# A fused sparse-attention and mixing kernel: the first batch's token sum in another order of terms, and the later weights' high parts rounded on ScalarE

## The chip, the cores and the metric

The kernel runs on one NeuronCore of a Trainium2 chip. The metric is the device time of one execution in microseconds (us). Before the change three executions took 988.09, 993.77 and 994.96 us (median 993.77). Engines are named as the profile names them: PE is TensorE, DVE is VectorE, ACT is ScalarE, POOL is GpSimd, SP is the engine that issues the DMAs.

## The reference, cut to what matters

```
# attention: 4 batches x 8 heads, 576 tokens, head dim 64
scores = q @ k.T / 8
kth = the 32nd largest score of each row
attn = softmax(scores where scores >= kth, else -1e9)
x = concat over heads (attn @ v)                  # 4 x 576 x 512

# first mixing block
theta = x @ w_theta
yr = einsum('ts,bsd->btd', w_tok_r, x * cos(theta))
yi = einsum('ts,bsd->btd', w_tok_i, x * sin(theta))
u = x + yr + yi                                   # "the token sum"
x = u + relu(u @ w_ch)

# second block
u, v = halves of relu(x @ w_in)
v = w_spatial @ layernorm(v) + b_spatial
out = (u * v) @ w_out
```

The weights of the first block and `w_in`, `w_out` arrive as 64-bit floats; q, k, v, `w_spatial` and `b_spatial` as 32-bit.

## The kernel before, in words

**Attention.** There are 16 visits (4 batches times 4 pairs of heads) of 9 tiles each, 144 tiles of 128 query rows by 576 keys. A tile goes through PE (`ps_s`, L429, two-part products), ACT (copy `x` out of PSUM, L433), DVE (the 32nd largest of each row, two tiles at a time: maximum and minimum of halves, L448 and L449, each with two inputs in SBUF, then MAX8 and MATCH_REPLACE8, L452 to L461, with one input), ACT (`sg` = Sign and `x` = Exp, L480 and L481), POOL (`sg` = their product, L482), PE (transpose `ps_t`, L491), ACT (`ptb`, L492) and PE (product with the values, `ps_v`, L513). Two tiles make a group; DVE is through a group in some 8.6 us while the weights are being split.

**The blocks behind it.** Each matrix product is made of three (`mm3`, L552 to L554): high part times high part, high times low, low times high, where the high part is the operand rounded to the matmul's type and the low part what is left. For the token sum, the sum over the 576 tokens is nine terms k of 128 rows: k = 0 to 3 are token tiles 0 to 3 of x·cos (tiles `zah`, `zal`; weights `tr`), k = 4 to 7 the same tiles of x·sin (`zbh`, `zbl`; weights `ti`), k = 8 the last 64 tokens of both (`zb`; weights `t9`). In the first batch, tiles 0, 1 and 2 go through `Front.rotate` first, and tiles 3 and 4 (the terms 3, 7 and 8) in a second call just before `middle`. The token sum has eight PSUM results (four channel chunks, two halves of the tokens), with three PSUM buffers `ps_m`.

**The weights.** `split_weights` loads each weight in parts, turns 64-bit words into 32-bit floats on DVE (L147, L148, L149; ACT's Abs at L150 and Sign at L154 test the range), rounds the high part (L193), subtracts it (L194) and writes both to DRAM (L204, L205). Seven larger parts of `th`, `tr`, `ti`, `t9` come first (`split_first`), then 21 parts of `ch`, `iv`, `iu`, `sp`, `s5`, `ou` with 512 or 576 columns (`split_rest`), of which 16 are 64-bit. They are recorded one to a group of attention tiles, and what is left after group 21 there. The blocks load each weight back into four large buffers `w` (L264); a load waits until the weight that held its buffer has been used for the last time in that batch.

**The order.** Work is recorded with priorities; a scheduler at build time then fixes one order of instructions for each engine. At run time each engine, and SP's queue of DMAs, goes through its list in that order.

Of the kernel before, what the change touches and what calls it, by code (L numbers as in the profile page):

```python
# [13 lines left out]
AF = mybir.ActivationFunctionType  # L14
OP = mybir.AluOpType
# [9 lines left out]
def sparse_attention_then_moe_kernel(  # L25
# [37 lines left out]
    NFIRST = 4  # L63
# [11 lines left out]
    act, dve, pool, pe = nc.scalar, nc.vector, nc.gpsimd, nc.tensor  # L75

    def f32(ap):
        return ap.bitcast(F32)
# [44 lines left out]
    def is_double(w):  # L123
        return w.dtype == mybir.dt.int64

    def words(w):

        return w.bitcast(I32).rearrange("k (n t) -> k n t", t=2)
# [11 lines left out]
    def double_to_f32(raw, f, exact, i):  # L140


        u = f.bitcast(I32)
        p, n = f.shape
        low, high = raw[:, :, 0], raw[:, :, 1]
        hf = high.bitcast(F32)
        dve.tensor_scalar(u, high, 3, 0x3FFFFFFF, op0=OP.logical_shift_left, op1=OP.bitwise_and)  # L147
        dve.scalar_tensor_tensor(u, low, 29, u, op0=OP.logical_shift_right, op1=OP.bitwise_or)  # L148
        dve.scalar_tensor_tensor(u, high, -(1 << 30), u, op0=OP.bitwise_and, op1=OP.bitwise_or)  # L149
        act.activation(hf, hf, AF.Abs)  # L150
        if exact:
            dve.scalar_tensor_tensor(f, hf, 2.0 ** -15, f, op0=OP.is_ge, op1=OP.mult)
        else:
            act.activation(hf, hf, AF.Sign, bias=smallest[0:p], accum_out=inside[0:p, 0, i:i + 1])  # L154
            pool.memset(inside[0:p, 1, i:i + 1], float(n))

    def split_weights(names, slots, step, exact, first):


        parts = []  # L160
        for n in names:
            parts += [(n, 0, 1)] if SIZE[n] == WID[n] else [(n, c, step) for c in range(0, 4, step)]

        def load(i):
            if i >= len(parts):
                return
            name, c, k = parts[i]
            raw, f, _ = slots[i % len(slots)]
            n = WID[name]
            if name == "t9":  # L170
                where = [(slice(0, 64), 0, w_rT[512:S]), (slice(64, 128), 0, w_iT[512:S])]
            elif name == "s5":
                where = [(slice(0, 64), 0, w_spT[512:S]), (slice(64, 65), 0, b_sp)]
            else:
                where = [(slice(0, 128), j, SRC[name][(c + j) * 128:(c + j + 1) * 128]) for j in range(k)]
            cols = slice(512, 1024) if name == "iv" else slice(0, n)
            for p, j, src in where:
                if is_double(src):
                    nc.sync.dma_start(raw[p, 2 * j * n:2 * (j + 1) * n].rearrange("p (n t) -> p n t", t=2),
                                      words(src)[:, cols])  # L180
                else:
                    nc.sync.dma_start(f[p, j * n:(j + 1) * n], src[:, cols])

        def finish(i):
            name, c, k = parts[i]
            n = k * WID[name]
            _, f, hi = slots[i % len(slots)]
            p = 65 if name == "s5" else 128
            f, hi = f[0:p, 0:n], hi[0:p, 0:n]
            if name == "th":  # L190

                pool.tensor_scalar(f, f, 1.0 / (2.0 * math.pi), 0.0, op0=OP.mult, op1=OP.add)
            pool.tensor_scalar(hi, f, 1.0, 0.0, op0=OP.mult, op1=OP.add)  # L193
            pool.tensor_tensor(f.bitcast(F32R), f, f32(hi), op=OP.subtract)  # L194
            hi = f32(hi)
            c = slice(c * WID[name], c * WID[name] + n)
            if name == "s5":
                for h in (slice(0, 64), slice(64, 128)):
                    nc.sync.dma_start(scratch[name, "h"][h], hi[0:64])
                nc.sync.dma_start(scratch[name, "l"][0:64], f[0:64])  # L200
                nc.sync.dma_start(scratch[name, "l"][64:65], hi[64:65])
                nc.sync.dma_start(scratch[name, "l"][65:66], f[64:65])
            else:
                nc.sync.dma_start(scratch[name, "h"][:, c], hi)  # L204
                nc.sync.dma_start(scratch[name, "l"][:, c], f)  # L205

        load(0)
        load(1)
        for i, (name, c, k) in enumerate(parts):
            yield  # L210
            raw, f, _ = slots[i % len(slots)]
            n = k * WID[name]
            src = {"t9": w_rT, "s5": w_spT}.get(name, SRC.get(name))
            if is_double(src):
                p = 65 if name == "s5" else 128
                double_to_f32(raw[0:p, 0:2 * n].rearrange("p (n t) -> p n t", t=2), f[0:p, 0:n],
                              exact, first + i)
            finish(i)
            load(i + 2)

    def split_first(exact):
        slots = []
        for raw, f in (("zah", "F"), ("zal", "zbh")):
            hi = wts.tile([128, 4 * S], F32R, name="w_hi", tag="w", bufs=WBUF)
            slots.append((big.tile([128, 4 * S], I32, name="w_raw", tag=raw),
                          big.tile([128, 4 * S], F32, name="w_f", tag=f), hi))
        return split_weights(ORDER[:NFIRST], slots, 2, exact, 0)

    def split_rest(exact):
        raw = big.tile([128, 2, 2 * S], I32, name="w_raw", tag="ph")  # L230
        f = big.tile([128, 4, S], F32, name="w_f", tag="pl")
        slots = [(raw[:, i], f[:, 2 * i], f[:, 2 * i + 1].bitcast(F32R)) for i in range(2)]
        return split_weights(ORDER[NFIRST:], slots, 1, exact, 10)

    ORDER = ["th", "tr", "ti", "t9", "ch", "iv", "iu", "sp", "s5", "ou"]

# [79 lines left out]
    def run(exact):  # L316
# [234 lines left out]
        def mm3(out, ah, al, bh, bl, first, last):  # L551
            pe.matmul(out, ah, bh, start=first, stop=False)  # L552
            pe.matmul(out, ah, bl, start=False, stop=False)  # L553
            pe.matmul(out, al, bh, start=False, stop=last)  # L554

        def mps(shape):
            return psum.tile(shape, F32, name="ps_m", bufs=3)
# [190 lines left out]
        FR = {}  # L748
# [28 lines left out]
        def middle(b):  # L777
# [7 lines left out]
            th, tl = (r + i + n for r, i, n in zip(*(W.get(b, n) for n in ("tr", "ti", "t9"))))  # L785
            for c in range(4):
                d = slice(c * 128, (c + 1) * 128)
                for m in halves:
                    p = mps([128, HALF])
                    for k in range(9):  # L790
                        mm3(p, *FR[b].z(k, d), th[k][:, m], tl[k][:, m], k == 0, k == 8)
                        if k == 4:
                            yield 1850
                    udve.tensor_tensor(F[:, c, m], p, F[:, c, m], op=OP.add)
                    lag.step(lambda c=c, m=m: ew.split(F[:, c, m], uh[:, c, m], ul[:, c, m]))
                    yield 1500
# [11 lines left out]
            first = True  # L808
            for m in halves:
                for e in range(4):  # L810
                    p = mps([128, HALF])
                    es = slice(e * 128, (e + 1) * 128)
                    if m is halves[1] and e == 0 or first:
                        lag.flush()
                        first = False
# [72 lines left out]
            for m in halves:  # L888
                for f in range(4):
                    fs = slice(f * 128, (f + 1) * 128)  # L890
                    p = mps([128, HALF])
# [34 lines left out]
        N = len(tiles)  # L926
        work = None
        conv = chain([split_first(exact), split_rest(exact)])
        preps = [iter(())]
        prep_first()  # L930
# [51 lines left out]
        def block(b):  # L982

            if b:
                gap = last(b - 1)
                yield from islice(gap, 4 if b == 1 else 0)
                yield from front(b)
                yield from gap
            else:
                yield from front(b)  # L990
            yield from middle(b)
# [79 lines left out]
```

## Time and profile before

| | |
|---|---|
| three runs | 988.09, 993.77, 994.96 us |
| profiled execution | 986.55 us, span 984.8 us |
| busy over the span | PE 87%, DVE 85%, ACT 64%, POOL 55% |
| DVE busy, 100 to 300 us (of 200) | 195.6 us |
| DVE idle before 800 us, after the start-up | some 26 us |
| DVE busy, 800 to 850 us (of 50) | 9.3 us |
| PE busy, 800 to 985 us (of 185) | 175.0 us |
| the 21 late parts are split | from 118 to 313 us |
| first batch's token sum | from 252 to 310 us |

An engine's busy time counts its instructions from start to end; where an instruction waits for something that no semaphore shows, the wait is inside its duration. The granted clock (PEclk) is a share of TensorE's full speed.

### The profile page before, as it was taken

What the parts mean: (1) busy time and instruction counts of PE and PEld (TensorE: products, weight loads), DVE (VectorE), ACT (ScalarE), POOL (GpSimd) and SP (SyncE); (2) the same over time, 40 slices, a digit from 0 to 9 for tenths busy, and PEclk for the clock granted to TensorE, in tenths of its full rate; (3) what the DMA queues carried; (4) which work ended last, traced back from release to release, by engine and by line L of the source; (5) the groups of instructions that cost most, each with busy time, mean ns of one, the idle gap of its engine ahead of it and who ended that gap; (6) DMA issues with size and microseconds to landing.
All of it is one profiled execution on the core that took longest, in us unless ns stands there. A gap on an engine that the chain in (4) does not pass through costs nothing.

```text
span 984.8 us, 17792 instructions
## 1 busy us (share of the span) xinstructions
PE 854.1 (87%) x5802; PEld 785.8 (80%) x5802; DVE 837.5 (85%) x2710; ACT 626.2 (64%) x1298; POOL 546.2 (55%) x476
## 2 busy tenths in 40 slices
PE   3656677785898999898998999799899999999997
PEld 2555666664797988897898998698889998889987
DVE  6999999899999998899999998999999951463552
ACT  5666767678767567777867777577957764350121
POOL 1686776658685854758385656375655553420030
PEclk9865676687899999999999999899999999999999
DMA  7797774647638463544461844352742645341221
GB/s 218 222 333 224 238 220 150 171 139 203 219 105 241 164 167 140 157 150 100 147 162 32 276 152 144 126 161 71 229 138 68 258 155 181 156 181 52 103 86 53
DMA packets 79393, 159.76 MB, mean 162 GB/s; under 512 B 36143, under 2 KB 40239, under 8 KB 71866
## 3 DMA queue, kind: packets, MB, share of 16 engines
q1 hardware_dynamic: 79290, 158.53, 51.0%
q8 instruction: 48, 0.79, 0.3%
q14 instruction: 55, 0.45, 0.1%
HBM read 108.63 MB, written 23.32 MB: 134 GB/s over the span
## 4 chain that ended last, share of the span: by engine, by line
DVE 46%; PE 32%; ACT 7%; DMA 7%; issue 4%; POOL 3%; SPq 1%; DVEq 0%; ACTq 0%; POOLq 0%
DVE mm L449 8%; PE ps_m L552 7%; DVE mx L458 7%; PE ps_m L553 7%; PE ps_m L554 7%; DVE mm L461 7%; DVE z L452 5%; DVE mm L448 4%; PE ps_v L513 4%; PE ps_s L429 2%; PE ps_t L491 2%; DVE F L568 2%; DMA q<-hi 2%; DVE z L448 2%; DVE cf L471 2%
## 5 line engine op out<-in xcount | busy, mean ns | idle before, releaser
L482 POOL TENSOR_TENSOR sg<-x,sg 128x576 f32<-128x576 f32 x144 | 213.0, 1495 | 150.9 <-ACT x L481 90.9
L513 PE MATMUL ps_v<-vc,ptb 128*128 128x65 f32 (+1 forms) x1280 | 176.6, 277 | 15.1 <-ACT ptb L492 15.1
L513 PEld LDWEIGHTS ps_v<-vc,ptb 128*128 128x128 f32 (+1 forms) x1280 | 167.4, 201 | 24.4 <-ACT ptb L492 18.5
L491 PE MATMUL ps_t<-ident,sg 128*128 128x128 f32 x648 | 132.0, 305 | 42.2 <-POOL sg L482 33.5
L480 ACT ACTIVATE sg<-x,cf 128x576 f32<-128x576 f32 x144 | 103.8, 769 | 56.0 <-DVE cf L471 53.2
L491 PEld LDWEIGHTS ps_t<-ident,sg 128*128 128x128 f32 x648 | 93.7, 166 | 53.9 <-POOL sg L482 39.0
L458 DVE MAX8 mx<-mm 128x8 f32<-128x160 f32 x432 | 118.9, 313 | 0.0
L433 ACT ACTIVATE x<-ps_s 128x576 f32<-128x576 f32 x144 | 92.4, 642 | 32.0 <-POOL sg L482 16.8
L429 PE MATMUL ps_s<-k,q 128*128 128x288 f32 x256 | 91.2, 367 | 24.1 <-ACT x L433 15.0
L552 PE MATMUL ps_m<-w_t,zah 128*128 128x288 f32 (+2 forms) x272 | 98.7, 363 | 11.3 <-DVE F L568 6.7
L481 ACT ACTIVATE x<-x,cf 128x576 f32<-128x576 f32 x144 | 108.0, 767 | 0.1
L492 ACT ACTIVATE ptb<-ps_t 128x640 f32<-128x640 f32 (+1 forms) x144 | 92.4, 642 | 13.2 <-PE ps_t L491 12.3
L554 PE MATMUL ps_m<-w_t,zal 128*128 128x288 f32 (+2 forms) x272 | 96.6, 355 | 0.6 <-DVE zal L568 0.4
L553 PE MATMUL ps_m<-w_t,zah 128*128 128x288 f32 (+2 forms) x272 | 96.5, 355 | 0.0
L452 DVE MAX8 z<-mm 128x8 f32<-128x312 f32 (+1 forms) x288 | 89.5, 372 | 1.9
L552 PE MATMUL ps_m<-w_t,zbh 128*128 128x288 f32 x288 | 85.9, 301 | 3.2 <-DVE F L568 1.9
L461 DVE MATCH_REPLACE8 mm<-mx,mm 128x160 f32<-128x160 f32 x288 | 87.0, 309 | 0.0
L553 PE MATMUL ps_m<-w_t,zbh 128*128 128x288 f32 x288 | 85.4, 300 | 0.6 <-DMA w_t<-d_spl 0.6
L554 PE MATMUL ps_m<-w_t,zbl 128*128 128x288 f32 x288 | 84.3, 299 | 1.0 <-POOL zbl L568 1.0
L552 PE MATMUL ps_m<-ph,w_t 128*128 128x288 f32 x256 | 76.8, 301 | 8.1 <-DMA w_t<-d_chh 4.3
L429 PEld LDWEIGHTS ps_s<-k,q 128*128 128x128 f32 x256 | 55.8, 218 | 33.1 <-ACT x L433 24.6
L449 DVE TENSOR_TENSOR mm<-x 128x576 f32<-128x576 f32 x72 | 82.2, 1141 | 0.0
(175 smaller groups left out, 2391.4 us busy)
## 6 DMA issues: line engine op xcount, KB each, us to landing
k<-hi SPq DMA_DIRECT2D x60, 144.0 KB, 2.6
kl<-raw SPq DMA_DIRECT2D x60, 144.0 KB, 3.1
vc<-in_v_dram SPq DMA_DIRECT2D x48, 128.0 KB, 2.8
w_t<-d_trh SPq DMA_DIRECT2D x4, 1152.0 KB, 5.2
w_t<-d_trl SPq DMA_DIRECT2D x4, 1152.0 KB
out_dram<-t SPq DMA_DIRECT2D x32, 144.0 KB, 2.2
raw<-in_q_dram SPq DMA_DIRECT2D x15, 288.0 KB, 3.0
q<-hi SPq DMA_DIRECT2D x30, 144.0 KB, 2.8
```

The costliest lines, as they stand in the source:

```text
L429: pe.matmul(o, q, k[:, m], start=a == 0, stop=a == len(terms) - 1)
L449: dve.tensor_tensor(mm[:, :, mid:hi], a, b, op=OP.min)
L452: dve.max(out=z[:, i, QUARTER + 8 * k:QUARTER + 8 * k + 8], in_=mm[:, i, losers])
L458: last = dve.max(out=top[i], in_=src[i])
L461: dve.match_replace(out=mr[i], in_to_replace=top[i], in_values=src[i], imm_value=NEG)
L481: act.activation(x, x, AF.Exp, bias=cf[:, 0:1], scale=0.125)
L482: pool.tensor_tensor(sg, x, sg, op=OP.mult)
L491: pe.transpose(pt[:, c, :], x[:, lo:lo + 128], ident)
L513: pe.matmul(o, pt[:, c, q], chunks[:, c, slot], start=alone and c == 0, stop=not alone and i == 1 and c == 3)
L552: pe.matmul(out, ah, bh, start=first, stop=False)
L553: pe.matmul(out, ah, bl, start=False, stop=False)
L554: pe.matmul(out, al, bh, start=False, stop=last)
```

## The change

In the first batch (`b == 0`) the nine terms of each PSUM result of the token sum are taken as 0, 1, 2, 4, 5, 6, 3, 7, 8; in the other batches as before. The generator hands back control after the sixth term instead of the fifth. For the 21 parts of `split_rest`, the rounding of the high part is an ACT activation (Copy) instead of a POOL tensor_scalar; the seven first parts stay on POOL.

```diff
-    def split_weights(names, slots, step, exact, first):
+    def split_weights(names, slots, step, exact, first, late):
...
-            pool.tensor_scalar(hi, f, 1.0, 0.0, op0=OP.mult, op1=OP.add)
+            if late:
+                act.activation(hi, f, AF.Copy)
+            else:
+                pool.tensor_scalar(hi, f, 1.0, 0.0, op0=OP.mult, op1=OP.add)
             pool.tensor_tensor(f.bitcast(F32R), f, f32(hi), op=OP.subtract)
...
-        return split_weights(ORDER[:NFIRST], slots, 2, exact, 0)
+        return split_weights(ORDER[:NFIRST], slots, 2, exact, 0, False)
...
-        return split_weights(ORDER[NFIRST:], slots, 1, exact, 10)
+        return split_weights(ORDER[NFIRST:], slots, 1, exact, 10, True)
...
-                    for k in range(9):
-                        mm3(p, *FR[b].z(k, d), th[k][:, m], tl[k][:, m], k == 0, k == 8)
-                        if k == 4:
+                    terms = range(9) if b else (0, 1, 2, 4, 5, 6, 3, 7, 8)
+                    for i, k in enumerate(terms):
+                        mm3(p, *FR[b].z(k, d), th[k][:, m], tl[k][:, m], i == 0, i == 8)
+                        if i == 5:
                             yield 1850
```

The scheduler makes another order of it on every engine. Line numbers of the changed kernel are higher by 4 to 6 from here on.

On POOL, around the fifth and sixth late part, the order before was this (`w_f` is the part, `sg` the attention's product):

```order
L193 TENSOR_SCALAR w_f<-w_f 128x512
L194 TENSOR_TENSOR w_f<-w_f 128x512
L482 TENSOR_TENSOR sg<-x,sg 128x576 x2
L193 TENSOR_SCALAR w_f<-w_f 128x512
L194 TENSOR_TENSOR w_f<-w_f 128x512
L482 TENSOR_TENSOR sg<-x,sg 128x576 x2
```

and now is:

```order
L486 TENSOR_TENSOR sg<-x,sg 128x576 x2
L198 TENSOR_TENSOR w_f<-w_f 128x512
L486 TENSOR_TENSOR sg<-x,sg 128x576
L198 TENSOR_TENSOR w_f<-w_f 128x512
L486 TENSOR_TENSOR sg<-x,sg 128x576 x3
```

The rounding is gone, and the subtraction, which stood ahead of its group's two products, now stands behind one or both of them.

On ACT, around the fifth late part, before:

```order
L480 ACTIVATE sg<-x,cf 128x576 x2
L481 ACTIVATE x<-x,cf 128x576
L492 ACTIVATE ptb<-ps_t 128x512
L150 ACTIVATE w_raw<-w_raw 128x512
L481 ACTIVATE x<-x,cf 128x576
```

and now:

```order
L484 ACTIVATE sg<-x,cf 128x576 x2
L437 ACTIVATE x<-ps_s 128x576
L485 ACTIVATE x<-x,cf 128x576 x2
L150 ACTIVATE w_raw<-w_raw 128x512
L195 ACTIVATE w_f<-w_f 128x512
L496 ACTIVATE ptb<-ps_t 128x512
```

The new copy (L195) stands behind the part's Abs (L150), here behind both Exp of the group; at the sixth part one Exp stands behind it.

On PE, at the first three results of the token sum, before (`w_t_1121` and `w_t_1123` are `tr`, `w_t_2418` and `w_t_2420` are `ti`), after the terms 0, 1, 2 of all three:

```order
L552 MATMUL ps_m_2764<-w_t_1121,zah_905 128x288
L553 MATMUL ps_m_2764<-w_t_1123,zah_905 128x288
L552 MATMUL ps_m_2616<-w_t_1121,zah_905 128x288
L553 MATMUL ps_m_2616<-w_t_1123,zah_905 128x288
L552 MATMUL ps_m_2725<-w_t_1121,zah_905 128x288
L553 MATMUL ps_m_2725<-w_t_1123,zah_905 128x288
```

and now, after the terms 0, 1, 2 of the first two:

```order
L556 MATMUL ps_m_2616<-w_t_2418,zbh_2263 128x288
L556 MATMUL ps_m_2725<-w_t_2418,zbh_2263 128x288
L495 MATMUL ps_t_2593<-ident_75,sg_2564 128x128
L557 MATMUL ps_m_2616<-w_t_2420,zbh_2263 128x288
L557 MATMUL ps_m_2725<-w_t_2420,zbh_2263 128x288
```

PE goes on with term 4, which needs the weights `ti`, where it took term 3, which needs token tile 3. The fourth result's first matmul stands at place 789 of PE's instructions before and 806 now; the first matmul with `ch` stands at place 1012 in both. Of the 5,059 instructions of PE in this pass 1,040 stand behind the last one of the attention, in both.

## Rows read from the trace of the kernel before

**Rows 1.** The page, part 1: busy us (share of the span) xinstructions.

```profile
PE 854.1 (87%) x5802; PEld 785.8 (80%) x5802; DVE 837.5 (85%) x2710; ACT 626.2 (64%) x1298; POOL 546.2 (55%) x476
```

**Rows 2.** Busy time by stretches; each number is busy us (xinstructions).

```profile
core 0: us, PE busy (x) PEld busy (x) DVE busy (x) ACT busy (x) POOL busy (x), PEclk, DMA share, GB/s
...
150.00:200.00 50.00, 38.23 (x182) 32.77 (x183) 46.96 (x169) 35.39 (x75) 30.80 (x26) 0.64 0.55 161
250.00:300.00 50.00, 45.83 (x333) 42.97 (x332) 49.27 (x153) 34.58 (x68) 37.23 (x35) 0.96 0.50 160
...
800.00:850.00 50.00, 49.18 (x340) 44.66 (x339) 9.27 (x45) 21.44 (x52) 21.44 (x23) 1.00 0.43 163
```

**Rows 3.** POOL's late parts: line 193 (ns min/median/max, first and last start us).

```profile
L193 POOL TENSOR_SCALAR w_f<-w_f x21: 608/758/1177, 120.5 to 307.4; 128x512 fp32r<-128x512 f32 x16, 128x576 fp32r<-128x576 f32 x4, 65x576 fp32r<-65x576 f32 x1
```

**Rows 4.** Groups of ACT, shapes apart: xcount | busy us, mean ns | idle before.

```profile
L568 ACT ACTIVATE zbh<-vt 128x512 fp32r<-128x512 f32 x12 | 7.3, 626 | 9.0 <-POOL vt L568 9.0
```

**Rows 5.** Timeline at the fifth late part: start us, us, engine, line; [idle before].

```profile
159.16 1.44 ACT L480 ACTIVATE sg<-x,cf 128x576 f32<-128x576 f32 x2 [1.01 <-DVE cf L471]
...
159.42 0.68 DVE L149 SCALAR_TENSOR_TENSOR w_f<-w_raw,w_f 128x512 int32<-128x512 int32 x1
...
160.19 0.76 POOL L193 TENSOR_SCALAR w_f<-w_f 128x512 fp32r<-128x512 f32 x1 [3.43 <-DVE w_f L149]
160.50 1.24 DVE L452 MAX8 z<-mm 128x8 f32<-128x312 f32 x4
160.51 0.76 ACT L481 ACTIVATE x<-x,cf 128x576 f32<-128x576 f32 x1
...
161.03 1.28 POOL L194 TENSOR_TENSOR w_f<-w_f 128x512 fp32r<-128x512 f32 x1
161.18 0.57 ACT L492 ACTIVATE ptb<-ps_t 128x512 f32<-128x512 f32 x1
161.66 0.67 ACT L150 ACTIVATE w_raw<-w_raw 128x512 f32<-128x512 f32 x1
...
162.26 2.77 POOL L482 TENSOR_TENSOR sg<-x,sg 128x576 f32<-128x576 f32 x2
...
165.56 0.76 DVE L448 TENSOR_TENSOR mm<-x 128x576 f32<-128x576 f32 x1
```

**Rows 6.** Timeline four groups earlier: POOL's products reach into DVE's L448.

```profile
123.52 2.95 POOL L482 TENSOR_TENSOR sg<-x,sg 128x576 f32<-128x576 f32 x2
...
125.14 1.95 DVE L448 TENSOR_TENSOR mm<-x 128x576 f32<-128x576 f32 x1
```

**Rows 7.** Groups of DVE from 120 to 250 us: xcount | busy us, mean ns | idle.

```profile
L449 DVE TENSOR_TENSOR mm<-x 128x576 f32<-128x576 f32 x11 | 11.0, 1000 | 0.0
L448 DVE TENSOR_TENSOR mm<-x 128x576 f32<-128x576 f32 x11 | 10.2, 924 | 0.0
```

**Rows 8.** The same groups from 311 to 800 us.

```profile
L449 DVE TENSOR_TENSOR mm<-x 128x576 f32<-128x576 f32 x46 | 54.1, 1176 | 0.0
L448 DVE TENSOR_TENSOR mm<-x 128x576 f32<-128x576 f32 x46 | 41.8, 908 | 9.1 <-ACT x L433 8.9
```

**Rows 9.** Busy time (columns as in Rows 2) as the token sum starts.

```profile
255.00:270.00 15.00, 11.29 (x77) 10.09 (x76) 14.89 (x56) 14.16 (x27) 8.40 (x10) 0.93 0.73 252
```

**Rows 10.** Timeline of SP's queue: loads of the weights ti (low) and ch.

```profile
258.40 0.32 SPq L264 DMA_DIRECT2D w_t<-d_til  x1
...
310.29 0.54 SPq L264 DMA_DIRECT2D w_t<-d_chh  x1
```

**Rows 11.** Timeline of PE: the first term 3, and the last use of tr.

```profile
268.94 0.59 PE L552 MATMUL ps_m<-w_t,zah 128*128 128x288 f32 x1
...
307.83 0.30 PE L554 MATMUL ps_m<-w_t,zal 128*128 128x288 f32 x1
```

**Rows 12.** PE's waits from 200 to 320 us: us in total, times, longest.

```profile
PE ps_m L552 <- DMA w_t<-d_chh: 3.9, 1, 3.9
```

**Rows 13.** DMA issues: xcount, KB each, median us to landing.

```profile
w_t<-d_til SPq DMA_DIRECT2D x3, 1152.0 KB, 8.6
```

## The prediction, made before the changed kernel was run

> **What bounds the kernel now.** I began with the page's busy shares: PE 87% and DVE 85% of the span, ACT 64%, POOL 55% [rows 1]. An average hides the stages, so I went on to busy time by stretches. From 250 to 300 us DVE is busy 49.27 us of 50, and from 150 to 200 us 46.96; from 800 us on DVE has 9.27 of 50 and PE 49.18 [rows 2]. So there are two parts: until about 800 us, while there is attention work, DVE has no idle time to speak of, and behind it PE works off what the last batches have left. The build's order says that 1,040 PE instructions stand behind the attention's last one before and after the change, so the second part is not touched by either edit, and the kernel gets faster only if DVE reaches its last group sooner.
>
> Then I looked for what DVE does with its time. L448 and L449 take 0.76 us where nothing disturbs them [rows 5], but their means are 0.92 and 1.00 us from 120 to 250 us, and 0.91 and 1.18 us from 311 to 800 us [rows 7, 8]. The timeline shows why: POOL's products run from 123.52 to 126.47 us, and the L448 that starts at 125.14 under them takes 1.95 us [rows 6]. DVE's instructions with two SBUF inputs stand still while POOL works. MAX8, with one input, does not: the one at 160.50 takes its 1.24 us for four while POOL is busy throughout [rows 5]. So POOL's work is free under DVE's MAX8 stretch of a group and dear beyond it.
>
> **Part one: the order of terms.** It removes and adds no instruction; it moves terms 3, 7 and 8 of each result behind 4, 5 and 6, so that PE need not wait for token tile 3 to be rotated. Term 3 began at 268.94 us [rows 11]. From 255 to 270 us PE is busy 11.29 us of 15 [rows 9], so 3.7 us is all that PE could win here. It will not have it all, since terms 4 to 6 need the weights `ti`, whose low part is issued at 258.40 us [rows 10] and takes a median of 8.6 us to land [rows 13]: 267.0 us, only 1.9 us before term 3 began. In the same 15 us DVE is busy 14.89 [rows 9]. DVE's group of attention tiles does not wait for the token sum, so PE's win has nothing to shorten. Bounds: a gain of 3.7 us, or nothing. I take 0, because DVE's row is nearly full; if DVE had gaps here, it would be the 1.9.
>
> The other side of this edit is the buffer of `tr`. Term 3 is its last use, and that use moves three terms, nine matmuls, later. At 11.29 us for 77 matmuls [rows 9] that is 1.3 us: from 307.83 [rows 11] plus its 0.30 to 309.4 us. The load of `ch`, which needs the buffer, is issued at 310.29 us [rows 10], because SP's queue comes to it only then. So this costs nothing while the queue is that late; if the queue were early, PE's wait of 3.9 us for `ch` [rows 12] would grow by at most 1.3 us, again under a busy DVE. The changed order of SP has the load behind the same copies of keys.
>
> **Part two: the rounding.** POOL loses 21 instructions of a median 0.758 us [rows 3], 15.9 us. ACT gains 21 copies; the nearest row, a copy of 128x512 to the same type, takes 0.626 us [rows 4], so 13.1 us. ACT is busy 35.39 us of 50 from 150 to 200 us [rows 2], so it has room for 0.63 us in each group. What counts is when POOL ends its share of the group. The fifth late part shows a regular group [rows 5]. DVE ends the part's last conversion at 159.42 + 0.68 = 160.10 us. POOL starts the rounding at once, at 160.19, subtracts from 161.03 and multiplies from 162.26 to 165.03. DVE's next L448 starts at 165.56: POOL clears the way with 0.53 us to spare.
>
> After the change POOL's share is 1.28 + 2.77 = 4.05 us instead of 4.84, but it can no longer start at 160.19. The product needs ACT's Exp, which ends at 160.51 + 0.76 = 161.27, and the subtraction needs the copy, which stands behind Abs. If POOL went on without a gap from 161.27, it would end at 165.32, still 0.24 us early: no cost. In the new order of the fifth part the copy out of PSUM stands ahead of the Exps. If it takes as long as the one that stood between them before, 0.57 us [rows 5], the Exps end at 161.84 and 162.60, Abs 0.67 later, the copy at 163.90; the products run from 161.84 to 164.61, the subtraction to 165.89: 0.33 us into L448. In the sixth part's order (one product, the subtraction, one product) the chain ends at the same 165.89. So a group costs 0 to 0.33 us. I take 0.3, since both orders that I worked out end there, for the 11 groups from 120 to 250 us [rows 7]: **+3.3 us**. In the groups from 250 to 311 us DVE also does the first batch's own work, and POOL's instructions do not fall so regularly; I take 0 there.
>
> On the other side, what can be won: the two rows of 120 to 250 us exceed the undisturbed 0.76 us by 11 x 0.24 + 11 x 0.16 = 4.4 us [rows 7]. If all of that came from POOL's rounding, the part would bring -4.4. I do not take it, because the rounding lies under L449's end and MAX8 [rows 5]. The copies of the split parts to DRAM wait for the subtraction as before, half a microsecond later, with nothing that waits for them soon: `ch`, the first of them, is read back at 310.29 [rows 10].
>
> The Trainium skill, SBUF — State Buffer, section Who interferes with whom, says that a DVE instruction with two SBUF inputs and a GpSimd instruction that reads SBUF exclude each other, and that the later one is held for the whole of the other. The 1.95 us agree with it [rows 6]. By the rule alone, each rounding taken from POOL could give back up to its whole length, 15.9 us in all.
>
> **The sum.** 986.55 us of the profiled execution, 0 for the terms, +3.3 for the rounding: 989.9 us. The profiled execution is the fastest of the four that are shown; their mean, with 988.09, 993.77 and 994.96, is 990.8, which is 4.3 us more. The change's runs I expect about as far above: 994 us, no change.
>
> **The rivals.**
> *Slower: ACT's copy comes late, and DVE is locked out for a whole product.* One product takes 2.77 / 2 = 1.39 us [rows 5]. If ACT, in order, reaches Abs and the copy one such step later, POOL's last instruction starts before 165.56 and holds L448 for most of its length. Eleven groups times 1.39 are 15.3 us: 986.55 + 15.3 + 4.3 = 1006. It decides when the copy ends after 164.6 us in the group shown, 0.7 later than I worked out. For it: the new copy waits for DVE and has attention work behind it, and POOL now waits twice on ACT in each group. Against it: ACT is idle some 30% there, and POOL has 0.76 us less to do. Chance 0.20.
> *Faster: the lock-outs shrink.* From 311 to 800 us L448 and L449 exceed 0.76 us by 46 x 0.42 + 46 x 0.15 = 26 us [rows 8], and the scheduler has dealt new orders there too. If the new order lets half of it go, that is -13: 978 us. For it: the excess is large and hangs on how POOL's and DVE's work fall together. Against it: nothing in the edit aims at that stretch; as much could be added. The rule above, at work on all 21 parts, would need 11 us of its 15.9 to come to the same side; the rounding would have to lie under L448, which the group shown does not have. Chance 0.15 together.
> *The terms' order works, and the rounding costs nothing:* -3.7 at most, 987 us. This is inside no change. Chance 0.10, which leaves 0.55 for the forecast.
>
> **How the numbers follow.** Three runs of one kernel lie 7 us apart, so less than 1% (10 us) can hardly be told from no change. Forecast and third rival together: within 1%, 0.65. Slower by over 1% 0.20, faster 0.15. The forecast's own range is 994 - 3.7 - 4.4 - 3.3 = 983 to 994 + 3.3 + 7 = 1004, the 3.3 being the unknown half of the rounding and the 7 the spread of runs. To leave out no more than two in ten I go to 980 and 1007, into the slower rival's time and towards the faster one's.
>
> **What would show it.** Busy time by stretches should show DVE within a microsecond of what it had from 250 to 300 us, and PE less idle from 255 to 270. In a group at 150 to 250 us POOL should be idle until the first Exp ends and should then end 0 to 0.4 us after the start of DVE's L448; L448's mean from 120 to 250 us should be 0.9 to 1.3 us. The time from DVE's last attention group to the end should stay what it is. I am wrong if that tail changes by more than 3 us, if L448 and L449 change their means from 311 to 800 us by more than 0.15 us, or if DVE shows new idle time ahead of the weights' conversions.

## The result, and the profile after

The changed kernel takes 998.9 us (median of 20 runs, 995.98 to 1004.04); the kernel before, on the same chip, 990.93 us (20 runs, 985.73 to 996.57). The ratio is 1.0074 [1.0058, 1.009]: slower by 0.74%, some 7.3 us (the medians are 8.0 us apart). It lies in the range and in "within 1%", to the slow side. The profiled span is 997.1 us against 984.8: the profiled execution of the kernel before is one of its fastest, so the two profiles lie 12.3 us apart, more than the medians.

The page after, part 1 (before: [rows 1]):

```profile
PE 859.0 (86%) x5802; PEld 790.4 (79%) x5802; DVE 835.2 (84%) x2710; ACT 637.8 (64%) x1319; POOL 526.9 (53%) x455
```

The work moved as intended: 21 instructions more on ACT, 21 fewer on POOL, and POOL has 19.3 us less to do. DVE's busy time fell by 2.3 us, so by this table the kernel has no reason to be slower (ACT has 11.6 us more, and has room). Busy time by stretches after (before: [rows 2, 9]):

```profile
core 0: us, PE busy (x) PEld busy (x) DVE busy (x) ACT busy (x) POOL busy (x), PEclk, DMA share, GB/s
150.00:200.00 50.00, 33.22 (x172) 28.40 (x172) 47.98 (x163) 35.79 (x77) 25.87 (x20) 0.69 0.53 149
250.00:300.00 50.00, 41.85 (x290) 38.93 (x289) 47.87 (x126) 37.90 (x73) 33.38 (x30) 0.93 0.58 184
800.00:850.00 50.00, 49.31 (x345) 44.94 (x345) 14.02 (x71) 25.40 (x60) 22.53 (x23) 1.00 0.52 193
255.00:270.00 15.00, 10.46 (x68) 10.11 (x69) 14.93 (x34) 12.56 (x24) 12.87 (x9) 0.89 0.87 301
```

From 250 to 300 us DVE is busy for nearly as long as before, but gets through 126 instructions instead of 153. A busy share does not tell work from standing still; a count beside it does. So I looked for places where both kernels had done the same work: numbers n for which the first n instructions of DVE are the same set in both, only in another order. This holds for 758, 928 and 1482, and but for 7 instructions for 1883. The changed kernel has done them at 260.0, 320.6, 493.5 and 612.3 us, the kernel before at 257.9, 310.7, 480.1 and 602.6. The lag grows by 2.1 us in the first 758 instructions and by 7.8 us in the next 170, then by 3.5, -3.7 and 2.6 us.

In those 170 instructions DVE's busy time went from 52.1 to 58.5 us and its idle time from 0.7 to 2.1 us. The four groups of DVE that grew most, in this stretch before (258 to 311 us; line, tile and shape, xcount | busy us, mean ns | idle before):

```profile
L149 DVE SCALAR_TENSOR_TENSOR w_f<-w_raw,w_f 128x512 int32<-128x512 int32 x4 | 3.1, 786 | 0.0
L448 DVE TENSOR_TENSOR z<-mm 128x288 f32<-128x288 f32 x4 | 2.4, 602 | 0.0
L471 DVE SCALAR_TENSOR_TENSOR cf<-cf,mx 128x2 f32<-128x2 f32 x4 | 2.2, 560 | 0.0
...
L465 DVE TENSOR_TENSOR flags<-z,mx 128x4 uint8<-128x4 f32 x4 | 1.3, 327 | 0.1
```

and the same groups after (260 to 321 us; here line numbers are 4 higher behind the weights):

```profile
L149 DVE SCALAR_TENSOR_TENSOR w_f<-w_raw,w_f 128x512 int32<-128x512 int32 x4 | 4.7, 1164 | 0.0
L452 DVE TENSOR_TENSOR z<-mm 128x288 f32<-128x288 f32 x4 | 3.8, 938 | 0.0
...
L469 DVE TENSOR_TENSOR flags<-z,mx 128x4 uint8<-128x4 f32 x4 | 3.4, 859 | 0.1
L475 DVE SCALAR_TENSOR_TENSOR cf<-cf,mx 128x2 f32<-128x2 f32 x4 | 3.2, 810 | 0.0
```

Equal instructions, the same number of them, longer: 15.1 us where it was 9.0; what the other groups gain and lose nearly cancels. One group of attention tiles shows why. Timeline after (start us, us, engine, line; [idle before]):

```profile
275.66 3.77 POOL L486 TENSOR_TENSOR sg<-x,sg 128x576 f32<-128x576 f32 x2 [2.10 <-ACT x L485]
...
276.71 0.79 DVE L469 TENSOR_TENSOR flags<-z,mx 128x4 uint8<-128x4 f32 x1
276.72 1.24 ACT L195 ACTIVATE w_f<-w_f 128x576 fp32r<-128x576 f32 x2
...
278.09 1.96 DVE L453 TENSOR_TENSOR mm<-x 128x576 f32<-128x576 f32 x1
...
279.40 3.51 POOL L198 TENSOR_TENSOR w_f<-w_f 128x576 fp32r<-128x576 f32 x2
...
279.97 1.67 DVE L452 TENSOR_TENSOR z<-mm 128x288 f32<-128x288 f32 x1
...
281.56 1.36 DVE L475 SCALAR_TENSOR_TENSOR cf<-cf,mx 128x2 f32<-128x2 f32 x1
```

POOL works from 275.66 to 289.54 us with no gap over 0.1 us, here first two products, then two subtractions. Both lie under DVE's instructions with two inputs; even `cf`, 128x2 values, takes 1.36 us. The Trainium skill, SBUF — State Buffer, section Who interferes with whom, has such a DVE instruction and one of GpSimd exclude each other for the whole of the other. The trace agrees: the second product ends at 279.43 us, the first subtraction at 281.33 and the second at 282.90, and `mm<-x` ends 0.62 us behind the first of these, `z<-mm` 0.31 us behind the second, `cf` 0.03 us behind the third. Undisturbed they take 0.75, 0.45 and 0.15 us, so each does its work when an instruction of POOL is through.

POOL is busy for longer than before in these 170 instructions, 42.8 us instead of 36.6, although the rounding is gone from it. Groups of POOL there, before:

```profile
L193 POOL TENSOR_SCALAR w_f<-w_f 128x512 fp32r<-128x512 f32 (+2 forms) x6 | 4.8, 795 | 2.2 <-issue 1.5 <-DVE w_f L149 0.6
L568 POOL TENSOR_TENSOR zbl<-xn,zbh 128x256 fp32r<-128x256 f32 x4 | 3.4, 859 | 0.0
```

and after:

```profile
L198 POOL TENSOR_TENSOR w_f<-w_f 128x512 fp32r<-128x512 f32 (+2 forms) x6 | 9.2, 1534 | 5.6 <-ACT w_f L195 3.8 <-DVE mx L462 1.9
L572 POOL TENSOR_TENSOR zbl<-xn,zbh 128x384 fp32r<-128x384 f32 (+1 forms) x8 | 8.5, 1092 | 0.0
L572 POOL TENSOR_TENSOR pl<-F,ph 128x288 fp32r<-128x288 f32 x6 | 5.5, 935 | 0.1
```

Six roundings (4.8 us) have left; four more splits of the sines (`zbl`) and six of the first batch's sum (`pl`), which had lain ahead of the stretch and behind it, are in it now: 5.1 + 5.5 us. Timeline of POOL around the stretch, before (it goes from 257.9 to 310.7 us):

```profile
248.23 4.40 POOL L568 TENSOR_TENSOR zbl<-xn,zbh 128x384 fp32r<-128x384 f32 x4
...
255.89 2.78 POOL L482 TENSOR_TENSOR sg<-x,sg 128x576 f32<-128x576 f32 x2 [0.84 <-ACT x L481]
...
318.92 6.97 POOL L568 TENSOR_TENSOR pl<-F,ph 128x288 fp32r<-128x288 f32 x7 [0.30 <-DMA d_oul<-w_f]
```

and after (from 260.0 to 320.6 us):

```profile
260.02 2.79 POOL L486 TENSOR_TENSOR sg<-x,sg 128x576 f32<-128x576 f32 x2 [0.87 <-ACT x L485]
262.77 5.23 POOL L572 TENSOR_TENSOR zbl<-xn,zbh 128x384 fp32r<-128x384 f32 x4
...
313.13 4.68 POOL L572 TENSOR_TENSOR pl<-F,ph 128x288 fp32r<-128x288 f32 x5
```

In POOL's list the four splits stood ahead of these two products, the 41st and 42nd, and now stand behind them; the first `pl` stood behind the 51st product and now stands behind the 48th. So they are in the stretch because the order at build time puts them there, not because POOL comes to them late. The subtractions wait 3.8 us for ACT's copies, in two places, and what POOL has behind them waits along.

DVE, too, has a wait there that the profile before does not show (us in total, times, longest; 250 to 320 us):

```profile
DVE w_f L147 <- DMA d_oul<-w_f: 1.9, 1, 1.9
```

### The profile page after: what moved, and what is told of

Its sections match the earlier page's. It is cut to its first block, busy times and chain, and to the rows that moved or that the text cites. A ratio compares the mean times of both kernels' runs of the same rounds, so it can differ in the third digit from the quotient of the medians.

```text
span 997.1 us, 17795 instructions
## 1 busy us (share of the span) xinstructions
PE 859.0 (86%) x5802; PEld 790.4 (79%) x5802; DVE 835.2 (84%) x2710; ACT 637.8 (64%) x1319; POOL 526.9 (53%) x455
## 4 chain that ended last, share of the span: by engine, by line
DVE 46%; PE 35%; ACT 8%; DMA 5%; issue 4%; POOL 1%; SPq 1%; DVEq 0%; ACTq 0%; POOLq 0%
PE ps_m L556 8%; PE ps_m L557 8%; PE ps_m L558 8%; DVE mx L462 7%; DVE mm L465 7%; DVE mm L453 7%; DVE z L456 5%; DVE mm L452 5%; PE ps_v L517 5%; PE ps_t L495 3%; PE ps_s L433 2%; DVE z L452 2%; DVE F L572 2%; DVE flags L469 2%; DVE st L572 1%
## 5 line engine op out<-in xcount | busy, mean ns | idle before, releaser
L517 PE MATMUL ps_v<-vc,ptb 128*128 128x65 f32 (+1 forms) x1280 | 179.9, 280 | 11.8 <-ACT ptb L496 11.8
L517 PEld LDWEIGHTS ps_v<-vc,ptb 128*128 128x128 f32 (+1 forms) x1280 | 169.9, 203 | 22.4 <-ACT ptb L496 14.4
L452 DVE TENSOR_TENSOR mm<-x 128x576 f32<-128x576 f32 x72 | 72.3, 1004 | 15.9 <-ACT x L437 15.5
L433 PE MATMUL ps_s<-kl,q 128*128 128x288 f32 x256 | 81.7, 330 | 0.0
```

Source lines behind the costliest of these rows:

```text
L433: pe.matmul(o, q, k[:, m], start=a == 0, stop=a == len(terms) - 1)
L452: dve.tensor_tensor(win[:, :, 0:mid], a, b, op=OP.max)
L517: pe.matmul(o, pt[:, c, q], chunks[:, c, slot], start=alone and c == 0, stop=not alone and i == 1 and c == 3)
```

## The experiments

Two accounts were held against each other: that the edits cost time by themselves, and that the order dealt anew on every engine, far behind the edits, does. So some kernels have one edit or a part, and some ("neutral") change only a number of the planner, so that the same instructions come in another order (from where on, stands below their table). All ratios are to the kernel before in the same job, with 95% intervals. The reading by equal work was made after all the runs, from their profiles; its table stands at the end of this section.

**The rounding alone.**

```diff
-            pool.tensor_scalar(hi, f, 1.0, 0.0, op0=OP.mult, op1=OP.add)
+            if first:
+                act.activation(hi, f, AF.Copy)
+            else:
+                pool.tensor_scalar(hi, f, 1.0, 0.0, op0=OP.mult, op1=OP.add)
```

> Only the rounding of the 21 late parts moves to ScalarE; the terms keep their order. Both edits together took +0.74% (+7.3 us). Theory A (the copy on ScalarE makes GpSimd's chain late, so that VectorE is held in each group): this kernel alone has +3 to +7 us, 3.3 us of it before 250 us as longer L448 and L449, and the rest as idle VectorE. Theory B (the edits cost next to nothing where they are; each makes the scheduler deal another order behind 250 us, and that order is what is slower): the 22nd attention group ends within 2 us of before, and the total can come out anywhere from -10 to +10 us, decided behind 250 us.

Measured: 997.18 us against 991.91, 1.0051 [1.0032, 1.007]. The rounding alone is slower by two thirds of what both edits cost; but the terms alone, next, are slower than both, so the parts do not add up.

**The terms' order alone.**

```diff
-                    for k in range(9):
-                        mm3(p, *FR[b].z(k, d), th[k][:, m], tl[k][:, m], k == 0, k == 8)
-                        if k == 4:
+                    terms = range(9) if b else (0, 1, 2, 4, 5, 6, 3, 7, 8)
+                    for i, k in enumerate(terms):
+                        mm3(p, *FR[b].z(k, d), th[k][:, m], tl[k][:, m], i == 0, i == 8)
+                        if i == 5:
```

> Only the order of the nine terms changes in the first batch; GpSimd rounds as before. Theory A: 0 us, at most -3.7 us by less idle TensorE from 255 to 270 us. Theory B: TensorE gains its 2 to 4 us there and the total is still anywhere from -10 to +10 us; nothing differs before 240 us.

Measured: 1002.81 us, 1.01 [1.0073, 1.0128]: slower than both edits together. Where the edit acts, it does what it is for. Busy time of this kernel as the token sum starts (columns as above; before: [rows 9]):

```profile
255.00:270.00 15.00, 11.77 (x82) 10.25 (x81) 14.85 (x47) 12.98 (x25) 10.89 (x13) 1.00 0.68 237
```

PE has 0.5 us less idle time than before. But DVE's 928th instruction ends at 313.4 us, among the neutral orders (310.7 to 316.5); the time is lost behind its 1482nd.

**No rounding at all, terms as before.** The part itself is taken as its high part, and POOL subtracts it from itself; the rounding of the 21 late parts is left out.

```diff
-            pool.tensor_scalar(hi, f, 1.0, 0.0, op0=OP.mult, op1=OP.add)
-            pool.tensor_tensor(f.bitcast(F32R), f, f32(hi), op=OP.subtract)
-            hi = f32(hi)
+            if first:
+                pool.tensor_tensor(hi, f, f, op=OP.subtract)
+                hi, f = f, f32(hi)
+            else:
...
```

> The rounding of the 21 late parts is left out: the part itself is written to DRAM as the high part, and GpSimd subtracts it from itself for the low part. GpSimd has 15.9 us less to do and ScalarE nothing more; nothing waits for ScalarE. Theory A: the opposite sign of the rounding on ScalarE: 0 to -4.4 us, with L448 and L449 shorter from 120 to 250 us. The rule of the exclusive port, if all rounding stood in VectorE's way: up to -15.9 us. Theory B: up to 250 us no more than 4 us gained, and a total from -10 to +10 us that does not follow from it.

Measured: 998.24 us, 1.0053 [1.0031, 1.0075]. By the total alone the rounding would be worth nothing. By equal work it is another thing: the 170 instructions take 52.2 us, 9.1 less than with the rounding alone on ACT (61.3), and POOL is busy 34.9 us there, where that kernel has 39.6 and the changed one 42.8. DVE's groups (264 to 316 us):

```profile
L149 DVE SCALAR_TENSOR_TENSOR w_f<-w_raw,w_f 128x512 int32<-128x512 int32 x4 | 3.9, 977 | 0.0
...
L452 DVE TENSOR_TENSOR z<-mm 128x288 f32<-128x288 f32 x4 | 1.8, 446 | 0.0
L475 DVE SCALAR_TENSOR_TENSOR cf<-cf,mx 128x2 f32<-128x2 f32 x4 | 1.2, 303 | 0.0
L469 DVE TENSOR_TENSOR flags<-z,mx 128x4 uint8<-128x4 f32 x4 | 1.0, 238 | 0.1
```

7.9 us, where the changed kernel has 15.1 and the one before 9.0. DVE is busy 48.1 us in all, 4.0 less than before, with no rounding on POOL or on ACT and in the order that was dealt for that. But DVE is idle 4.1 us here, so little of it is kept.

**Only the parts of `ch` and `iv` on ACT** (8 of 21).

```diff
-            pool.tensor_scalar(hi, f, 1.0, 0.0, op0=OP.mult, op1=OP.add)
+            if name in ("ch", "iv"):
+                act.activation(hi, f, AF.Copy)
+            else:
+                pool.tensor_scalar(hi, f, 1.0, 0.0, op0=OP.mult, op1=OP.add)
```

> Only the first 8 of the 21 late parts (ch and iv) are rounded on ScalarE. Theory A: 8/21 of the rounding's cost, +1 to +3 us. Theory B: not in proportion; the build's order leaves 10% more matmul columns behind the last attention tile than before (361 thousand against 328 thousand), so that the tail is some 13 us longer, and attention ends earlier by an unknown part of that; total from -5 to +13 us.

Measured: 1015.97 us, 1.0227 [1.0196, 1.0259]. A smaller edit, three times the loss. Its last copy on ACT starts at 194.9 us; POOL rounds every part that is split behind 258 us, and waits for no copy. Yet the 170 instructions take 61.6 us, and POOL is busy 40.7 us in them. No edited instruction runs in the stretch here. So neither copies in the stretch nor waits for them are needed for the loss; what this kernel shares with the slow ones is that eight `zbl` and some `pl` fall into the stretch. Its list has the first four `zbl` ahead of the 41st product, as before the change, but POOL has come two products less far when the stretch begins. Most of its loss lies elsewhere: 1,294 PE instructions stand behind DVE's last attention group, 1,204 before the change, and that tail takes 205.4 us instead of 187.4. What of that is the edit's and what the order's, I can't say.

**Neutral orders, and both edits on each of them.** The planner's credit for a group (`QUOTA`) or the group behind which all parts that are left are recorded (`SPLIT`), one of them in each kernel; further kernels have a credit of 1980 and of 2020:

```diff
-    FIRST_QUOTA, QUOTA = 2500, 2000
+    FIRST_QUOTA, QUOTA = 2500, 2010
...
-    SPLIT = 21
+    SPLIT = 22
```

> The kernel before with one number changed that only steers the recording: the credit per half step, 2000 to 2010. No instruction is added, removed or moved to another engine; only the order is dealt anew (PE's list keeps about three quarters of its places, and 315,649 instead of 328,449 matmul columns stand behind the last attention tile). Theory A (the work that the two edits move is what costs): within 2 us of before. Theory B (any new order costs, since the old one was the best of many that were tried): +3 to +15 us, with idle VectorE behind 250 us.

> The same with the credit at 1980 instead of 2000; 297,569 matmul columns behind the last attention tile. Theory A: within 2 us of before. Theory B: +3 to +15 us; the tail is some 10 us shorter than before and the attention ends by more than that later.

> Both edits of the change, and the credit at 2010. Theory A: as the change itself, +7 us over before, within 2 us. Theory B: not tied to the change's time; anywhere from -3 to +15 us over before.

> Both edits of the change, and the last weight parts are all recorded at group 22 instead of 21 (SPLIT), so the conversions of the last parts come one group later. Theory A: +7 us over before, within 2 us, or less by up to 1.9 us if the wait of the conversion at 297 us for the store of an earlier part goes. Theory B: anywhere from -3 to +15 us over before.

> The kernel before with SPLIT 22 instead of 21: the partner of the run with both edits and SPLIT 22 (+0.87%). What the pairs decide: Theory A (the edits have a cost of their own): the partner with both edits is slower by 4 to 9 us in every pair. Theory B (only the order dealt counts): the differences within pairs have both signs and scatter by as much as the runs without an edit do, 16 us from the lowest to the highest so far. Alone: -5 to +13 us against before under B, within 2 us under A.

> Both edits and the credit at 1980; partner of the run with the credit at 1980 alone (+1.18%, 1003.8 us). Theory A: 4 to 9 us above the partner, 1008 to 1013 us. Theory B: anywhere from 990 to 1010 us, as likely below the partner as above it. In the trace the 37th attention group ends 4 to 8 us later than in the partner (438.4 us), as in the two pairs looked at.

> The kernel before with the credit at 2020, nothing else. Theory A: within 2 us of before. Theory B: -5 to +13 us. Being the next step from 2010, which was 0.36% faster than before, it may also be faster than both.

> Both edits and the credit at 2020; partner of the run with the credit at 2020 alone. Theory A: 4 to 9 us above the partner. Theory B: the sign is open. The 37th attention group ends 4 to 8 us later than in the partner in either case, if the rounding's cost in the first third is real.

Measured (us; ratio to the kernel before):

| order | without the edits | with both | difference |
|---|---|---|---|
| as it was | 990.93 | 998.9, 1.0074 [1.0058, 1.009] | +0.74% |
| credit 2010 | 987.26, 0.9964 [0.9938, 0.9989] | 1001.09, 1.0099 [1.0066, 1.0132] | +1.35% |
| credit 1980 | 1003.84, 1.0118 [1.0083, 1.0152] | 1012.1, 1.02 [1.0173, 1.0227] | +0.82% |
| credit 2020 | 989.3, 0.9975 [0.9955, 0.9995] | 1011.52, 1.0201 [1.0167, 1.0234] | +2.26% |
| split 22 | 993.86, 1.0008 [0.9992, 1.0023] | 999.77, 1.0087 [1.0054, 1.012] | +0.79% |

Without any change of work the order alone is worth 16.6 us (987.26 to 1003.84). And on each setting of the planner the edits cost time, 1.2% or some 12 us in the mean. But the settings separate the two accounts less than they seem to. Set side by side by operation, tiles and shape, the instructions of the kernels with another credit come on every engine and in SP's queue in the order of the kernel that they were made from, until some 350 us with credit 1980 and 460 us with 2010 and 2020; with `SPLIT` 22 they do so to the end. That number altered nothing (no conversion came a group later), and its row is a second measurement of the first. So there are four orders and not five, and until 350 us all five pairs hold one and the same pair of orders.

Where the order's share lies, the profiles show by equal work. The two widest apart of the neutral ones, credit 2010 and credit 1980, are 3 us apart at DVE's 1883rd instruction, at 608.6 and 605.7 us, and the one that is later there ends 18 us earlier. Groups of DVE from 610 to 795 us, credit 2010:

```profile
L449 DVE TENSOR_TENSOR mm<-x 128x576 f32<-128x576 f32 x18 | 20.5, 1137 | 0.0
...
L471 DVE SCALAR_TENSOR_TENSOR cf<-cf,mx 128x2 f32<-128x2 f32 x18 | 5.5, 303 | 0.4 <-ACT cf L470 0.4
```

and credit 1980:

```profile
L449 DVE TENSOR_TENSOR mm<-x 128x576 f32<-128x576 f32 x16 | 26.9, 1679 | 0.0
...
L471 DVE SCALAR_TENSOR_TENSOR cf<-cf,mx 128x2 f32<-128x2 f32 x15 | 9.3, 620 | 0.8 <-ACT cf L470 0.7
```

It is the same lock-out: half of L449's instructions take 0.85 us or less in the one order, and half 1.97 or more in the other. Behind the 1883rd instruction DVE's two-input instructions with no operand in PSUM take 119.6 us with credit 2010 and 143.2 with 1980, 23.6 us more, where the stretch is 20.9 us longer.

**All kernels by equal work.** Length of the stretches between DVE's instructions, in us, each from one profile:

| | to 758 | 758 to 928 | 928 to 1482 | 1482 to 1883 | to the end |
|---|---|---|---|---|---|
| before | 257.9 | 52.8 | 169.4 | 122.5 | 382.2 |
| credit 2010 | 257.9 | 53.5 | 173.4 | 123.7 | 375.8 |
| credit 1980 | 261.7 | 53.7 | 170.5 | 119.8 | 396.7 |
| credit 2020 | 260.8 | 53.5 | 169.6 | 125.4 | 378.1 |
| split 22 | 262.1 | 54.4 | 173.1 | 121.1 | 387.2 |
| **mean of these** | **260.1** | **53.6** | **171.2** | **122.5** | **384.0** |
| after | 260.0 | 60.6 | 172.9 | 118.8 | 384.8 |
| both, 2010 | 266.1 | 60.8 | 169.1 | 119.4 | 384.8 |
| both, 1980 | 264.5 | 60.9 | 170.8 | 119.5 | 398.9 |
| both, 2020 | 262.6 | 61.2 | 170.4 | 121.4 | 395.3 |
| both, split 22 | 261.8 | 60.4 | 170.3 | 119.1 | 385.6 |
| **mean of these** | **263.0** | **60.8** | **170.7** | **119.6** | **389.9** |
| rounding alone | 262.6 | 61.3 | 166.2 | 124.8 | 379.4 |
| terms alone | 260.4 | 53.0 | 170.3 | 125.8 | 390.5 |
| no rounding | 263.9 | 52.2 | 168.5 | 120.5 | 394.6 |
| 8 parts on ACT | 262.8 | 61.6 | 169.0 | 125.4 | 396.3 |

(The sets of instructions differ by at most 3; at 1883 by 7 in two kernels with both edits and by 15 in the last row.) How far one execution's profile can be trusted is seen in "before" and "split 22", the same order twice: their stretches differ by 4.2, 1.6, 3.7, 1.4 and 5.0 us.

In one column the kernels fall apart without an overlap: from 758 to 928 every one with copies on ACT takes 60.4 to 61.6 us, every one without 52.2 to 54.4. That is far beyond the 1.6 us, but it is no count of eight kernels against seven. The five with both edits have one order there, and the rounding alone has it too until some 265 us; the five neutral ones have one order, and the terms alone have it until some 267 us. Only "no rounding" and "8 parts on ACT" bring others.

POOL's busy time in the stretch is longer in the slow kernels (38.6 to 42.8 us against 34.9 to 36.6), but so is the stretch: as a share it is 63 to 71% against 66 to 69% and parts nothing. What parts them is where POOL's work lies. DVE has 49 two-input instructions with no operand in PSUM here. They take 32.3 to 35.7 us with copies on ACT and 28.3 to 29.2 without (24.2 with no rounding), and POOL works during 20.0 to 25.2 us of them against 12.9 to 16.0. In the mean of the five pairs these 49 make 4.1 of the 7.2 us, and DVE's idle time 1.6.

The last column, in which no edited instruction runs, scatters over 21 us among the neutral ones. The difference of the two means, 12.6 us, is 2.9 + 7.2 - 0.5 - 2.9 + 5.9. The first column's two sets overlap, the 2.9 us less in the fourth appear in every pair (0.3 to 4.3), and the last difference is under a third of its column's scatter. To the 1883rd instruction the pairs are 0.9 to 10.0 us apart, 6.7 in the mean.

**A version that beats both** is the neutral order with credit 2010, 987.26 us: 0.36% under the kernel before, for the price of one number. Credit 2020 comes near it (0.25%). Neither says that a higher credit is better, since the orders around them scatter as widely; each is a lucky order among the few that were tried.

## Why the prediction was right, and where it was wrong

**The verdict** (no change by 1%, to the slow side) was right, with a loss for the rounding as forecast. That the total came out near the forecast is in good part luck: the largest loss lies in a stretch that was put at 0, and another order of the same work moves the total by more than all the terms.

**The terms: 0.** Right for the stretch where they act. PE wins 0.5 us of the 3.7 that were the bound when this edit is alone, and DVE's 928th instruction comes no earlier. With both edits PE from 255 to 270 us is even less busy, 10.46 us of 15: what was to be seen there was not. In all, the kernel with the terms alone lost 1.0%, most of it behind 480 us, in an order that the forecast had no term for.

**The rounding until 250 us: +3.3.** The size fits, but that it is the rounding's is not shown: to DVE's 758th instruction, near 260 us, the mean of the five pairs is +2.9 us, with 2.1 in the profiled pair. The single pairs go from -0.3 to 8.2, and one and the same order differs by 4.2 us from execution to execution; the kernel with no rounding at all, and no copies, comes as late (263.9 us). The forms of DVE from 120 to 250 us after (before: [rows 7]):

```profile
L452 DVE TENSOR_TENSOR mm<-x 128x576 f32<-128x576 f32 x12 | 12.7, 1060 | 0.1
L453 DVE TENSOR_TENSOR mm<-x 128x576 f32<-128x576 f32 x12 | 11.8, 986 | 0.0
```

L448's successor has the 0.9 to 1.3 us that I asked for. The two together grew by 12 x 0.136 - 12 x 0.014 = 1.5 us. The fifth part's group looks as worked out, but for its end:

```profile
160.26 0.68 DVE L149 SCALAR_TENSOR_TENSOR w_f<-w_raw,w_f 128x512 int32<-128x512 int32 x1
...
161.29 1.43 ACT L485 ACTIVATE x<-x,cf 128x576 f32<-128x576 f32 x2
...
162.13 2.78 POOL L486 TENSOR_TENSOR sg<-x,sg 128x576 f32<-128x576 f32 x2 [4.52 <-ACT x L485]
162.62 0.66 ACT L150 ACTIVATE w_raw<-w_raw 128x512 f32<-128x512 f32 x1
163.18 0.62 ACT L195 ACTIVATE w_f<-w_f 128x512 fp32r<-128x512 f32 x1
...
164.86 1.28 POOL L198 TENSOR_TENSOR w_f<-w_f 128x512 fp32r<-128x512 f32 x1
...
166.40 0.75 DVE L452 TENSOR_TENSOR mm<-x 128x576 f32<-128x576 f32 x1
```

POOL is idle until the first Exp ends. The copy ends 2.86 us after the part's last conversion, 0.9 sooner than I had it, since that conversion now comes 1.5 us behind the start of the Signs and not 0.9; and POOL ends at 166.14, 0.26 us ahead of L452, where I had it 0.33 us late. So this group costs nothing. The 0.3 us in each of 11 groups is not what happened; L448 and L449 together give 1.5 us, of 2.1 in the profiled pair.

**"In the groups from 250 to 311 us ... I take 0 there."** This is the step that failed. The 170 instructions there cost 7.2 us in the mean of the pairs (6.0 to 7.8 each), twice the whole term that I had. Of these 5.6 us are longer instructions of DVE and 1.6 us idle time. The sentence ahead of it held the reason: POOL's instructions fall less regularly there, and I took "not regular" for "free". The slower rival had half of the mechanism, DVE locked out, but by a late POOL at the 11 regular groups, at 15.3 us; it happened at four irregular ones, where the build's order puts the first batch's own splits on POOL. DVE's busy share, for which I asked to stay within a microsecond, fell by 1.4 us there, and the wait that I had named as a sign of error appeared: a conversion waits 1.9 us for the store of the part that held its buffer. The kernel before's own order has that wait too, in four of its five profiles (1.3 to 2.3 us in the neutral ones), so it is not the rounding's price.

**Behind 311 us: no change, and the tail.** L448 and L449 kept their means from 311 to 800 us within my 0.15 (before: [rows 8]):

```profile
L453 DVE TENSOR_TENSOR mm<-x 128x576 f32<-128x576 f32 x47 | 49.8, 1060 | 0.0
L452 DVE TENSOR_TENSOR mm<-x 128x576 f32<-128x576 f32 x47 | 46.1, 981 | 13.5 <-ACT x L437 13.3
```

Measured from DVE's last attention group the tail grew from 187.4 to 191.5 us, over my 3 us. But PE works under it in another order; at 800 us PE's equal work lags by 12.1 us and at the end by 12.0, so the stretch itself adds nothing. My sign was badly chosen: a stretch that begins at a group of attention doesn't hold the same work in two orders. The same trap caught me in the runs. Counted by attention groups, the five kernels with both edits lose 6.1 us between the 37th group and the 53rd (without an overlap), where no edited instruction runs; counted by equal work nothing is lost there. The group had come early, not the work late.

**The sum.** I added 4.3 us to the profiled execution and 3.3 for the edit. The stretch that I took at 0 cost 7.2 us in the mean of the pairs, some 3 came back from 1482 to 1883, and what lies behind that can't be told from the order's scatter. A forecast of one build can be no better than the scatter of the orders; that what the order adds could be as large as every term of the sum was only in the rivals, with 13 us for one side.

**What stays open.** That from 758 to 928 POOL works under more of DVE's two-input instructions, and that these are held by it, the rows show in every kernel with copies on ACT. Whether the edits cost this by themselves is not shown. With both edits it is the order dealt at build time that brings four `zbl` and six `pl` into the stretch. With 8 parts on ACT the same loss comes with no edited instruction in the stretch; with no rounding, where POOL has as little to do, five `pl` fall into it and nothing is lost. So neither the amount of POOL's work nor copies in the stretch decide it. What the waits for copies add (3.8 us of POOL after the change, 5.4 with the rounding alone) is open: no run moved the copies with the rest of the order held. And only the terms alone had another order in this stretch with the rounding unmoved, from some 267 us on, and lost nothing there; one such order is too few. The stretches are from one profile each.

## What to carry to other kernels

Taking work from an engine that is not full can go with longer work on one that is: what counts is not how much the helper works but under which instructions of the bound engine its work falls, and a new wait or order moves that. Where a scheduler deals the order anew with every edit, time a few builds in which no work changes, and the edit on each of them, before you believe a difference of 1%. Look up in the traces from where on their orders differ: a build that is the same up to the place in question says nothing about it. Compare profiles at equal work, by sets of instructions, and never at the n-th group.

## What the runs showed of the hardware

The lock-out of DVE by POOL is larger than I had it for short instructions: `cf<-cf,mx`, 128x2 elements, takes 0.15 us when POOL rests and 1.36 us under a subtraction of POOL. It is not confined to two-input instructions either: the TENSOR_SCALAR `rs<-xr`, 128x10, takes 0.17 us before the change, where POOL rests, and after it 0.90 us under a subtraction, with which it ends (310.07 and 310.04 us). Over a stretch it hangs on the order alone: L449, one and the same instruction, took a mean of 1.14 us in one neutral order and 1.68 in another, from 610 to 795 us.
